# Batch 0 of a packed-attention and mixture-of-experts kernel: K loaded first and in four pieces, gate weights as rows turned on the chip, chunk 0 of the first layer ahead of the second piece of packed weights

## The chip, the cores and the metric

The kernel runs on one core of one Trainium2 chip. The metric is the device time of one execution in microseconds (us), as the median of several runs. The engines of a core are named as the profile names them: PE is TensorE's matrix products and PEld its weight loads, DVE is VectorE, ACT is ScalarE, POOL is GpSimd, SP is SyncE, which issues most DMAs. An engine with a q behind its name (SPq, ACTq) is that engine's instruction queue, where DMAs are issued.

## What is computed

Eight batches, eight heads, 576 tokens, head size 64. Attention goes twice through 32 packed rows per head; its output, 512 wide, goes through one of eight experts for each token. Which expert it is follows from a gate; a token can also keep the expert of the token before it.

```python
def _attn_ref(q, k, v, p):
    scale = 1.0 / np.sqrt(q.shape[-1])
    def sm_attn(qq, kk, vv):
        s = scale * np.matmul(qq, kk.transpose(0, 1, 3, 2))
        s = s - np.max(s, axis=-1, keepdims=True)
        a = np.exp(s)
        a = a / (np.sum(a, axis=-1, keepdims=True) + 1e-09)
        return np.matmul(a, vv)
    p_packed = sm_attn(p, k, v)
    out = sm_attn(q, p_packed, p_packed)
    return out.astype(np.float32)
...
    logits = np.einsum('bsd,de->bse', x, w_gate)
    local_gate = 1.0 / (1.0 + np.exp(-np.einsum('bsd,de->bse', x, w_local).squeeze(-1)))
...
            fresh_e = int(np.argmax(logits[b, s]))
            if s == 0 or local_gate[b, s] < 0.5:
                e = fresh_e
            else:
                e = prev_e if prev_e >= 0 else fresh_e
...
            h = np.maximum(x[b, s] @ w1[e], 0.0)
            out[b, s] = p[e] * (h @ w2[e])
```

## The kernel before

The kernel takes it that all tokens of a batch use the expert of the batch's first token, and works out at the end whether any did not; for these there is a general branch, which doesn't run here. For each batch it computes the packed rows (`ppT`, two groups Q of four heads), multiplies them into w1 of the expert ("packed weights", `pack_weights`), and then runs the two layers over eight chunks c of 128 hidden columns and two parts of the tokens (256 and 320 columns). Each float32 product in the layers is made of three: every operand is split into a high part and the rest (`wph` and `wpl`, `a2h` and `a2l`, the two halves of `w2s`).

Work is written as generators, one for each step of each batch. A planner (`weave`, with a cost table in the class `Clock`) runs the program's steps in the order in which its own estimate of the engines' times lets them be ready, and each `yield need(...)` names the tiles, buffers, banks or conditions on which a step waits. The order on each engine is fixed by this when the program is built; on the chip each engine runs its list in order and waits on semaphores. So a change of one condition or one estimate shifts places throughout the program. All loads go out on SP in the order of `loads`. They use eight completion semaphores in turn, so the ninth DMA waits for the first to have landed.

Batch 0 is special (`early`). Its start, in the program's order:

- `loads` (L355): p, K in two halves (`load_whole`, L284), the first rows of q for three batches (`t`), V in two groups, the gate weights (`w`: `wgl`, 64 partitions x 8 heads x 8 or 1 numbers, loaded in this layout straight from DRAM), Q in two halves.
- Five products of a zero tile (L227, 256 columns each: `WARM`) keep TensorE at work till the data is there; more of them are put in wherever the planner sees PE idle ahead of batch 0's first chunk.
- p is turned (L413), then K in six groups of three 128x128 transpositions (`turn_whole`, L439), whose copies out of PSUM (L440) alternate between ACT and DVE. Then come the scores (L447), maxima, exponentials (L550), their transpositions (L567), the products with V (L598), and two transpositions of the packed rows (`zz`, L616), each with a copy to `ppT` on ACT (L619).
- The probe of the first token (`early_choice`): a product of `ppT` with the first rows of q for each group (L870), a small softmax, a product with the gate values (L903), the largest of eight (L908, L910). SP reads the expert's number (L855) and issues that expert's weights: two pieces of the first half of w1 (`w1k`, 256 columns each, L1025), four chunks of w2 (L1032), then the second half of w1 (`w1t`).
- Meanwhile Q is turned (L439, L440, tile `qT`) and the second attention step runs in two parts of the tokens (`first_queries`).
- `pack_weights` multiplies `ppT` into w1 (L1073), in pieces of `w1k` and then `w1t`; ACT casts the high part (L1082), DVE makes the rest (L1085). Chunks 0 and 1 need the first `w1k` piece, 2 and 3 the second, 4 to 7 `w1t`. The first layer's products are at L1101, the second layer's at L1153.

## Time and profile before

| | us |
|---|---|
| median of 3 runs (413.15 to 414.97) | 413.54 |
| the profiled execution | 414.13 |
| its span, first to last instruction | 412.3 |
| PE busy in the span | 400.5 (97%) |
| DVE, ACT, POOL busy | 247.8, 188.3, 110.5 |

The span is what the profile's rows cover; the 1.8 us between it and the profiled execution's time lie around it. PE is nearly always busy, so the place to look for is where it is not, and what the chain of waits, followed back from the last instruction, names there. Matrix products are pipelined and their ends are modelled; the distance between starts says more than the duration of one. A row of the timeline merges neighbours with the same operation: its first number is the start, the second the time that they take together, and "x" their number, where a float32 product of more than one pass counts as two. What stands in brackets is the engine's idle time before it and what ended it.

### The profile page before, as it was taken

How to read it: one execution, taken by the hardware profiler on the slowest of the kernel's cores; microseconds unless marked ns; L12 is line 12 of the kernel's file. 1: busy time of each engine (PE TensorE's matmuls, PEld its weight loads, DVE VectorE, ACT ScalarE, POOL GpSimd, SP SyncE). 2: the span in 40 equal slices, each digit the busy share in tenths (PEclk: the TensorE clock that was granted, in tenths of full speed). 3: DMA queues.
4: the chain of work that ended last, by engine and by line, in shares of the span. 5: the costliest groups of instructions: out<-in, count | busy, mean ns of one | idle time of the engine just before them, and what ended most of it. 6: DMA issues, size and time to landing. Idle time of an engine off the chain costs nothing.

```text
span 412.3 us, 9812 instructions
## 1 busy us (share of the span) xinstructions
PE 400.5 (97%) x3724; PEld 317.4 (77%) x3725; DVE 247.8 (60%) x666; ACT 188.3 (46%) x447; POOL 110.5 (27%) x138
## 2 busy tenths in 40 slices
PE   8988999999999999999999999999999999999993
PEld 6766777777877788678887887778868788778883
DVE  4697468783877587758934697248842595332221
ACT  2574524744346532485344643545344643453212
POOL 1014500912055203036304412323303413233000
PEclk9999999999999999999999999999999999999998
DMA  7899679974699299569994994899175102820102
GB/s 230 249 313 229 97 187 368 157 173 125 215 274 207 73 220 184 192 231 222 213 334 139 187 200 138 306 229 213 51 248 163 61 4 88 324 93 22 52 0 68
DMA packets 161053, 72.98 MB, mean 177 GB/s; under 512 B 131186, under 2 KB 139882, under 8 KB 161002
## 3 DMA queue, kind: packets, MB, share of 16 engines
q1 hardware_dynamic: 160858, 72.19, 67.8%
q8 instruction: 30, 0.49, 0.5%
q14 instruction: 21, 0.17, 0.1%
q10 hardware_dynamic: 144, 0.13, 0.1%
HBM read 62.87 MB, written 9.44 MB: 175 GB/s over the span
## 4 chain that ended last, share of the span: by engine, by line
PE 91%; DMA 4%; SPq 1%; ACT 1%; DVE 1%; issue 1%; DVEq 0%; ACTq 0%
PE bank L1153 43%; PE bank L1101 24%; PE bank L1073 4%; DMA w1t<-in_moe_w_dram 4%; PE bank L1159 4%; PE bank L1163 3%; PE bank L598 2%; PE bank L567 2%; PE bank L647 2%; PE bank L508 1%; PE bank L227 1%; PE bank L922 1%; PE bank L439 1%; PE bank L616 1%; SPq L1032 0%
## 5 line engine op out<-in xcount | busy, mean ns | idle before, releaser
L1153 PE MATMUL bank<-w2s,h 128*128 128x512 f32 (+1 forms) x771 | 203.8, 397 | 0.0
L1153 PEld LDWEIGHTS bank<-w2s,h 128*128 128x128 f32 x771 | 136.0, 188 | 30.7 <-issue 7.6
L1116 DVE SCALAR_TENSOR_TENSOR h<-bank,h 128x256 fp32r<-128x256 f32 x192 | 61.8, 350 | 98.6 <-ACT h L1112 97.7
L1133 POOL TENSOR_TENSOR w2s<-w2raw,w2s 128x512 fp32r<-128x512 f32 (+1 forms) x68 | 84.2, 1255 | 134.2 <-ACT w2s L1129 127.2
L1112 ACT ACTIVATE h<-bank 128x320 fp32r<-128x320 f32 (+1 forms) x128 | 53.0, 414 | 107.8 <-PE bank L1101 106.0
L1101 PEld LDWEIGHTS bank<-a2h,wph 128*128 128x128 f32 x256 | 46.2, 188 | 18.3 <-issue 5.1
L1101 PE MATMUL bank<-a2h,wph 128*128 128x256 f32 (+1 forms) x256 | 56.6, 302 | 0.0
L1101 PE MATMUL bank<-a2l,wph 128*128 128x256 f32 (+1 forms) x256 | 54.9, 295 | 0.0
L1101 PE MATMUL bank<-a2h,wpl 128*128 128x256 f32 (+1 forms) x256 | 54.6, 295 | 0.0
L1101 PEld LDWEIGHTS bank<-a2l,wph 128*128 128x128 f32 x256 | 40.9, 188 | 0.0
L1101 PEld LDWEIGHTS bank<-a2h,wpl 128*128 128x128 f32 x256 | 40.9, 188 | 0.0
L710 POOL TENSOR_TENSOR a2l<-a2t,a2h 128x320 fp32r<-128x320 f32 (+1 forms) x25 | 20.6, 843 | 75.0 <-ACT a2h L704 75.0
L1129 ACT CAST w2s<-w2raw 128x512 fp32r<-128x512 f32 x64 | 38.7, 620 | 0.8 <-DMA w2raw<-in_moe_w_dram 0.6
L1085 DVE TENSOR_TENSOR wpl<-bank,wph 128x512 fp32r<-128x512 f32 (+1 forms) x34 | 21.2, 651 | 19.8 <-ACT wph L1082 19.8
L1082 ACT CAST wph<-bank 128x512 fp32r<-128x512 f32 (+1 forms) x34 | 17.4, 565 | 24.5 <-PE bank L1073 24.4
L1159 PE MATMUL bank<-w2s,h 128*128 128x512 f32 x64 | 26.4, 412 | 0.0
L1163 PE MATMUL bank<-w2s,h 128*64 128x512 f32 x64 | 25.1, 392 | 0.0
L1193 ACT ACTIVATE o<-bank,pe 128x512 f32<-128x512 f32 x23 | 15.5, 700 | 8.6 <-PE bank L1153 8.5
L634 DVE STREAM_TRANSPOSE qn<-qn 128x1152 f32<-128x1152 f32 x14 | 19.2, 1369 | 0.0
L1073 PE MATMUL bank<-w1t,ppT 64*32 64x512 f32 x240 | 17.0, 601 | 1.7 <-DMA w1t<-in_moe_w_dram 1.7
L460 DVE STREAM_TRANSPOSE qn<-qn 128x1152 f32<-128x1152 f32 x12 | 16.4, 1363 | 0.0
L569 ACT COPY a1T<-bank 116x384 f32<-116x384 f32 (+1 forms) x29 | 11.8, 432 | 9.4 <-PE bank L567 9.4
(150 smaller groups left out, 382.1 us busy)
## 6 DMA issues: line engine op xcount, KB each, us to landing
w2raw<-in_moe_w_dram SPq DMA_DIRECT2D x64, 256.0 KB, 7.5
w1t<-in_moe_w_dram SPq DMA_DIRECT2D x15, 1024.0 KB, 5.1
kv<-in_v_dram SPq DMA_DIRECT2D x16, 560.0 KB, 7.5
qn<-in_q_dram SPq DMA_DIRECT2D x28, 288.0 KB, 4.8
out_dram<-o SPq DMA_DIRECT2D x31, 256.0 KB, 2.7
qn<-in_k_dram SPq DMA_DIRECT2D x24, 288.0 KB, 4.3
raw<-in_k_dram SPq DMA_DIRECT2D x4, 576.0 KB
raw<-in_q_dram SPq DMA_DIRECT2D x2, 576.0 KB
```

The costliest lines, as they stand in the source:

```text
L634: nc.vector.transpose(out=qT, in_=qT)
L710: engine.tensor_tensor(out=a2l[:, cols], in0=a2t[:, cols], in1=a2h[:, cols].bitcast(F32), op=ALU.subtract)
L1073: nc.tensor.matmul(out=ts[Q][32 * h:32 * h + 32, :width], lhsT=st["ppT"][Q][rows, 32 * h:32 * h + 32], rhs=w1t[rows, h], start=True, stop= ...
L1085: nc.vector.tensor_tensor(out=lo[:, Q, cols], in0=ts[Q][:, :width], in1=hi[:, Q, cols].bitcast(F32), op=ALU.subtract,)
L1101: nc.tensor.matmul(out=t[:, :width], lhsT=st["wp"][c // 4][wi][:, Q, fs], rhs=a2[ai][Q][:, ts], start=(n == 0), stop=(n == 5),)
L1112: nc.scalar.activation(out=h[:, :n], in_=t[:, :n], func=AF.Relu)
L1116: nc.vector.scalar_tensor_tensor(out=h[:, dst:dst + z - a], in0=t[:, a:z], scalar=0.0, in1=h[:, a:z].bitcast(F32), op0=ALU.max, op1=ALU.su ...
L1129: nc.scalar.copy(out=w[:, 0], in_=raw)
L1133: rest.tensor_tensor(out=w[:, 1, cols], in0=raw[:, cols], in1=w[:, 0, cols].bitcast(F32), op=ALU.subtract)
L1153: nc.tensor.matmul(out=acc[:, cols], lhsT=hs[hi], rhs=w[:, wi, cols], start=(c == 0 and n == 0), stop=(n == 2 and (c == NC - 1 or c == NC ...
L1159: nc.tensor.matmul(out=acc, lhsT=h[:, EDGE:EDGE + 2 * TAIL], rhs=w[:, 0], start=(c == 0), stop=False, skip_group_check=True,)
L1163: nc.tensor.matmul(out=acc[0:TAIL], lhsT=h[:, EDGE:EDGE + TAIL], rhs=w[:, 1], start=False, stop=(c == NC - 1), skip_group_check=True,)
```

## The change

For batch 0 alone:

- SP loads K first, in four pieces: groups 0 to 2, then 3, 4 and 5 alone. p, the gate weights and the first rows of q are loaded on ACT's queue instead, ahead of ACT's table load. The gate weights come as eight rows of 512 (and of 64) numbers, as they lie in DRAM, and nine transpositions on PE and one copy on DVE (`local_weights`) bring them into the old layout.
- Three warm-up products, not five, and the planner's estimates of when PE and the first DMA are free are lowered.
- Q's first three groups may be turned before the probe is done, and turning starts once the first group of packed rows has its transposed exponentials.
- The first chunk's products are placed ahead of the products of the second `w1k` piece, which now wait (in the planner) for that chunk. The maxima of the second part of the tokens wait for the third chunk.

```diff
@@ -42,10 +42,10 @@
 
 FIRST_BACKLOG = 1400.0
 
-WARM, FILL, EACH = (256,) * 5, 0.8, 1.8
+WARM, FILL, EACH = (256,) * 3, 0.8, 1.8
 
 LAT, SAME = 160.0, 127.0
-START, FIRST_LOAD = 6100.0, 1700.0
+START, FIRST_LOAD = 4300.0, 1300.0
 KEPT = ("bank6", "bank7")
 BUFS = {
     "kv": 2, "qn": 3, "p_in": 2, "q_in": 1, "zz": 2, "a1": 2, "a1T": 2, "a1U": 2, "ppT": 3, "sT": 2, "a2t": 2,
@@ -281,13 +281,13 @@
         ready.banks = banks
         return ready
 
-    def load_whole(src, b):
+    def load_whole(src, b, cuts=(0, NG // 2, NG)):
 
         x = tile_([128, NG, NM * 2 * D], F32, "raw", "qn")
-        clock.edges[x.tensor.name] = (H * HALF // 2,)
+        clock.edges[x.tensor.name] = tuple(NM * 2 * D * g for g in cuts[1:-1])
         clock.rate = 400.0
         rows = src[b].rearrange("h s d -> (h s d)").rearrange("(p g x) -> p g x", p=128, g=NG)
-        for z in (slice(0, NG // 2), slice(NG // 2, NG)):
+        for z in (slice(*y) for y in zip(cuts, cuts[1:])):
             nc.sync.dma_start(out=x[:, z], in_=rows[:, z])
         return x
 
@@ -355,9 +355,14 @@
 
         b = st["b"]
         if st["early"]:
-            st["p"] = load_packs_whole(b, nc.sync)
+            st["p"] = load_packs_whole(b, nc.scalar)
+            st["rows"] = tile_([H, D * GW], F32, "rows", "w2s")
+            nc.scalar.dma_start(out=st["rows"][:, :D * E], in_=w_gate.rearrange("(h d) e -> h (d e)", d=D))
+            nc.scalar.dma_start(out=st["rows"][:, D * E:], in_=w_local.rearrange("(h d) e -> h (d e)", d=D))
+            st["t"] = tile_([FIRST * H, D], F32, "q_in")
+            nc.scalar.dma_start(out=st["t"], in_=q[0:FIRST, :, 0].rearrange("b h d -> (b h) d"))
             nc.scalar.activation(out=spare_col, in_=ones_col, func=AF.Exp)
-            order = (("k", 0), ("t", 0), ("v", 0), ("v", 1), ("w", 0), ("q", 0))
+            order = (("k", 0), ("v", 0), ("v", 1), ("q", 0))
         else:
             if isinstance(b, int):
                 yield need(when=lambda: "loaded" in sts[b - 1] and (b < 2 or "ereg" in sts[b - 2]) and (b <= FIRST or len(sts[b - 2].get("w2", ())) == NC))
@@ -371,16 +376,6 @@
 
                 yield need(when=lambda: len(sts[b - 1].get("w1", ())) == 2)
             room = "p_in" if name == "p" else "qn" if name in "kq" else "kv"
-            if name == "t":
-                st["t"] = tile_([FIRST * H, D], F32, "q_in")
-                clock.rate = 100.0
-                nc.sync.dma_start(out=st["t"], in_=q[0:FIRST, :, 0].rearrange("b h d -> (b h) d"))
-                continue
-            if name == "w":
-                clock.rate = 20.0
-                nc.sync.dma_start(out=wgl[:, :, 0:E], in_=w_gate.rearrange("(h d) e -> d h e", d=D))
-                nc.sync.dma_start(out=wgl[:, :, E:E + 1], in_=w_local.rearrange("(h d) e -> d h e", d=D))
-                continue
             if st["whole"] and name == "q":
                 yield need(when=lambda: "turning" in st)
             if ends is None or name != "v":
@@ -400,7 +395,7 @@
                 if Q:
                     st[name] = True
             else:
-                st["raw" + name] = load_whole(x, b)
+                st["raw" + name] = load_whole(x, b, *(((0, 3, 4, 5, 6),) if st["early"] and name == "k" else ()))
         st["loaded"] = True
 
     def turn_packs(st):
@@ -426,13 +421,13 @@
 
         yield need(when=lambda: "raw" + name in st)
         raw = st["raw" + name]
-        yield need(slot="qn", when=lambda: name == "k" or "rawk" in sts[1])
+        yield need(slot="qn")
         x = tile_([128, NG, H, HALF // NG], F32, name + "T", "qn")
         st["turning"] = True
         clock.edges[x.tensor.name] = tuple(H * HALF // NG * g for g in range(1, NG))
         for g in range(NG):
             yield need(raw[:, g], banks=1, when=lambda: (
-                (name == "k" or g == 0 or "spread" in st) if st["early"] else g < 3 or sts[0]["raised"] > 0
+                (name == "k" or g < 3 or "spread" in st) if st["early"] else g < 3 or sts[0]["raised"] > 0
             ))
             tp = bank()
             for m in range(NM):
@@ -624,7 +619,7 @@
     def turn_queries(st, Q):
         if st["early"]:
             if Q == 0:
-                yield need(when=lambda: st.get("probed", 0) > 0)
+                yield need(when=lambda: ("turned", 0) in st)
                 act, dve = nc.scalar.copy, nc.vector.tensor_copy
                 yield from turn_whole(st, "q", (act, act, act, dve, act, act))
             return
@@ -751,7 +746,7 @@
                     give(ts[Q, 0], ts[Q, 1])
 
         def highest(z):
-            yield need(sT[z]) if z == 0 else need(when=lambda: st["packed"] > 256)
+            yield need(sT[z]) if z == 0 else need(when=lambda: st["firsts"] > 2)
             nc.vector.reduce_max(out=mx[z], in_=sf[z], axis=AX.X)
 
         def raised(z):
@@ -823,10 +818,21 @@
         for x in (*st["a2t"], *st["a2h"], *st["a2l"]):
             clock.edges[x.tensor.name] = (EDGE,)
 
+    def local_weights(st):
+
+        yield need(st["rows"], banks=1)
+        tp = bank()
+        for e in range(GW):
+            rows = st["rows"][:, e:D * E:E] if e < E else st["rows"][:, D * E:]
+            nc.tensor.transpose(out=tp[:D, H * e:H * e + H], in_=rows, identity=ident[:H, :H])
+        nc.vector.tensor_copy(out=wgl[:, :, 0:GW], in_=tp[:D, :H * GW].rearrange("a (e h) -> a h e", h=H))
+        give(tp, st["rows"])
+        st["local"] = True
+
     def gate_weights(st):
 
-        yield need(when=lambda: None not in st["ppT"])
-        yield need(*st["ppT"], banks=1)
+        yield need(when=lambda: None not in st["ppT"] and "local" in sts[0])
+        yield need(*st["ppT"], wgl, banks=1)
         gp = bank()
         for Q in range(NQ):
             for h in range(HQ):
@@ -1065,7 +1071,7 @@
                 if isinstance(st["b"], int) and st["b"] == B - 1 and fh:
                     yield need(w1t)
                     yield from look_for_strays()
-                yield need(w1t, banks=NQ, skip=skip, left=1)
+                yield need(w1t, banks=NQ, skip=skip, left=1, when=lambda: not (early and fh == 0 and n) or st["firsts"] > 0)
                 ts = [bank(skip=skip) for Q in range(NQ)]
                 for Q in range(NQ):
                     rows = slice(64 * Q, 64 * Q + 64)
@@ -1245,8 +1251,9 @@
             hi, lo = st["wp"][c // 4]
             cols = slice(*EDGES[part:part + 2])
             fs = slice(128 * (c % 4), 128 * (c % 4) + 128)
-            packs = [x[:, Q, fs] for x in (hi, lo) for Q in range(NQ)]
-            rests = () if st["early"] and part == 0 and c == 0 else st["a2l"]
+            soon = st["early"] and part == 0 and c == 0
+            packs = [x[:, Q, fs] for x in ((hi,) if soon else (hi, lo)) for Q in range(NQ)]
+            rests = () if soon else st["a2l"]
             yield need(*packs, *(x[:, cols] for x in (*st["a2h"], *rests)), banks=1)
             h, done = tile_([128, S + TAIL], F32R, "h"), set()
             aside(relu(layer1(c, part, st), part, h, done))
@@ -1317,7 +1324,7 @@
                 st = sts[started]
                 threads.extend(Thread(g, started) for g in (
                     slots(st), pack_weights(st), *((early_choice(st),) if st["first"] else ()),
-                    turn_keys(st, 0), turn_keys(st, 1), *((scores(st, 0), scores(st, 1)) if st["whole"] else (scores(st, 0, 1),)), keys(st, 0), keys(st, 1), gate_weights(st) if st["first"] else None, gates(st), turn_queries(st, 0), turn_queries(st, 1), first_queries(st) if st["early"] else queries(st, beside(started)),
+                    turn_keys(st, 0), turn_keys(st, 1), *((local_weights(st),) if st["early"] else ()), *((scores(st, 0), scores(st, 1)) if st["whole"] else (scores(st, 0, 1),)), keys(st, 0), keys(st, 1), gate_weights(st) if st["first"] else None, gates(st), turn_queries(st, 0), turn_queries(st, 1), first_queries(st) if st["early"] else queries(st, beside(started)),
                 ) if g is not None)
                 threads.insert(0, Thread(weights(st), started, True))
                 threads.append(Thread(splits(st), started, True))
```

How this moves instructions is decided by the planner. Three places follow. Lines from 281 on shift a little in the new kernel: L439 becomes L434, L413 L408, L619 L614, L440 L435, L1101 L1107, L1073 L1079, L556 L551.

PE from its first product to the first group of K, before: `warm` is the zero tile, `p_in` is p, `raw` is K as loaded.

```order
L227 MATMUL bank_66<-warm 128x256 x5
L413 MATMUL bank_126<-ident,p_in 128x128 x2
L439 MATMUL bank_135<-ident,raw 128x128 x3
L439 MATMUL bank_140<-ident,raw 128x128 x3
L439 MATMUL bank_145<-ident,raw 128x128 x3
```

And after, where `rows` are the gate weights as loaded:

```order
L227 MATMUL bank_66<-warm 128x256 x3
L408 MATMUL bank_127<-ident,p_in 128x128 x2
L827 MATMUL bank_136<-ident,rows 64x8 x9
L227 MATMUL bank_66<-warm 128x128
L434 MATMUL bank_148<-ident,raw 128x128 x3
```

Two warm-up products of 256 columns are gone; nine small transpositions and one warm-up product of 128 columns stand between p and K.

ACT around the two copies of the packed rows and the probe, before: `ppT` are the packed rows, `qT` is a turned group of Q, `es` the probe's exponentials.

```order
L569 COPY a1T<-bank_230 116x384
L619 COPY ppT<-bank_295 128x128
L619 COPY ppT<-bank_299 128x128
L440 COPY qT<-bank_307 128x384
L887 ACTIVATE es,em<-es,em 128x32
L842 COPY gate_90<-bank_316 128x64
```

And after:

```order
L564 COPY a1T<-bank_244 116x384
L614 COPY ppT<-bank_309 128x128
L435 COPY qT<-bank_312 128x384
L435 COPY qT<-bank_317 128x384
L614 COPY ppT<-bank_326 128x128
L435 COPY qT<-bank_329 128x384
L893 ACTIVATE es,em<-es,em 128x32
L848 COPY gate_88<-bank_338 128x64
```

Two copies of Q have moved between the two copies of the packed rows; on PE the same two groups of Q stand between the transpositions that feed them.

ACT in the first batch's second part of the tokens, around the exponentials of batch 1's scores (`a`), before:

```order
L556 ACTIVATE a_473,s_773<-a_473,nb 128x576
L569 COPY a1T<-bank_777 116x384
L1112 ACTIVATE h<-bank_760 128x320
L569 COPY a1T<-bank_783 116x256
L965 ACTIVATE ex<-under 128x40
L967 ACTIVATE fresh_all<-lt 128x5
L556 ACTIVATE a_714,s_800<-a_714,nb 128x576
```

And after:

```order
L551 ACTIVATE a_486,s_776<-a_486,nb 128x576
L564 COPY a1T<-bank_783 116x384
L564 COPY a1T<-bank_790 116x256
L551 ACTIVATE a_731,s_798<-a_731,nb 128x576
L971 ACTIVATE ex<-under 128x40
L973 ACTIVATE fresh_all<-lt 128x5
L1118 ACTIVATE h<-bank_801 128x320
```

The second exponential has moved ahead of a relu (`h`) and two small activations.

## Rows read from the trace of the kernel before

**Rows 1.** Busy time by stage: stretch, PE, PEld, DVE, ACT, POOL busy, clock, DMA.

```profile
33.70:406.00 372.30, 371.26 (x3363) 295.31 (x3363) 224.99 (x596) 169.77 (x398) 104.24 (x117) 1.00 0.68 171
```

**Rows 2.** The chain of waits, 0 to 60 us: start, us, what it was.

```profile
6.37 2.03 PE bank L439 x18
...
9.16 0.70 PE bank L447 x16
...
24.05 9.56 DMA w1t<-in_moe_w_dram
...
33.66 1.09 PE bank L1073 x16
```

**Rows 3.** Timeline, 26 to 34 us: start, us, engine, line, operation, tiles.

```profile
26.90 0.74 DVE L797 TENSOR_TENSOR a2l<-a2t,a2h 128x256 fp32r<-128x256 f32 x2
...
26.93 0.67 PE L1073 MATMUL bank<-w1k,ppT 64*32 64x256 f32 x16 [0.99 <-DMA w1k<-in_moe_w_dram]
...
33.66 1.09 PE L1073 MATMUL bank<-w1t,ppT 64*32 64x512 f32 x16 [1.16 <-DMA w1t<-in_moe_w_dram]
```

**Rows 4.** Timeline, 15 to 19.6 us, the probe of the first token.

```profile
15.54 0.27 ACT L619 COPY ppT<-bank 128x128 f32<-128x128 f32 x1 [1.26 <-PE bank L616]
...
16.08 0.27 ACT L619 COPY ppT<-bank 128x128 f32<-128x128 f32 x1 [0.28 <-PE bank L616]
...
16.65 0.26 PE L870 MATMUL bank<-ppT,q 64*32 64x32 f32 x8
...
16.81 0.48 ACT L440 COPY qT<-bank 128x384 f32<-128x384 f32 x1 [0.46 <-PE bank L439]
...
18.33 0.21 DVE L894 STREAM_TRANSPOSE et<-es 128x32 f32<-128x32 f32 x1
...
18.75 0.28 PE L903 MATMUL bank<-gate,et 128*1 128x32 f32 x4
...
19.07 0.16 DVE L908 MAX8 emx<-bank 1x8 f32<-1x8 f32 x1
```

**Rows 5.** Timelines of PE and of its weight loads, 3 to 9 us.

```profile
3.60 1.91 PE L227 MATMUL bank<-warm 128*128 128x256 f32 x4
4.46 1.49 PE L227 MATMUL bank<-warm 128*128 128x256 f32 x3
...
5.74 0.23 PEld L413 LDWEIGHTS bank<-ident,p_in 128*128 128x128 f32 x1 [0.20 <-issue]
5.95 0.23 PEld L439 LDWEIGHTS bank<-ident,raw 128*128 128x128 f32 x1
...
6.16 2.23 PE L439 MATMUL bank<-ident,raw 128*128 128x128 f32 x18
```

**Rows 6.** Line 477, q's first rows turned: duration ns min/median/max, first and last start.

```profile
L477 PEld LDWEIGHTS bank<-ident,q_in x1: 105/105/105, 8.3 to 8.3; 24*64 24x64 f32 x1
```

**Rows 7.** Busy time by stage while K is loaded; the last number is GB/s.

```profile
2.00:4.70 2.70, 2.70 (x8) 2.13 (x7) 0.78 (x3) 0.34 (x2) 0.00 (x0) 1.00 0.86 246
2.00:6.20 4.20, 4.20 (x13) 3.24 (x12) 0.78 (x3) 0.34 (x2) 0.00 (x0) 1.00 0.92 297
```

**Rows 8.** Timeline: the first DMAs, p's first copy, and ACT's one DMA.

```profile
0.88 0.45 SPq L343 DMA_DIRECT2D p_in<-in_p_dram  x1
1.38 0.94 SPq L291 DMA_DIRECT2D raw<-in_k_dram  x2
...
2.95 0.23 DVE L409 COPY p_in<-p_in 128x128 f32<-128x128 f32 x1 [0.48 <-DMA p_in<-in_p_dram]
...
407.10 0.39 ACTq L1176 DMA_DIRECT2D out_dram<-o  x1
```

**Rows 9.** Timeline, 48 to 50 us, batch 1's second exponential and its user.

```profile
48.66 0.78 ACT L556 ACTIVATE a<-a,nb 128x576 f32<-128x576 f32 x1
...
49.59 0.81 PE L567 MATMUL bank<-ident,a 128*116 128x128 f32 x5 [0.55 <-ACT a L556]
```

**Rows 10.** The page's DMA issues: KB each, median us from issue to landing.

```profile
w1t<-in_moe_w_dram SPq DMA_DIRECT2D x15, 1024.0 KB, 5.1
```

## The prediction

> **What bounds the kernel now.** I first read where TensorE (PE) stands idle, since everything else is fed to it. From 33.70 to 406.00 us PE is busy 371.26 of 372.30 us [rows 1]: that stretch is a wall of matrix products, which the change reorders but doesn't shorten. What comes ahead of it can be shortened. The chain of waits shows what opens the wall: the load of the second half of the first expert's w1 (w1t), issued at 24.05 and in use 9.56 us later, at 33.66 [rows 2]. PE had run out of other work 1.16 us before [rows 3]. So a microsecond is won only if that load is issued earlier, or if idle time inside the wall goes. The load is issued as soon as SyncE (SP) has the number of the first token's expert, and this number comes out of a chain: load K and p, turn them (L439), scores, softmax, products with V, the probe of the first token (L870), the largest gate value (MAX8, L908, at 19.07 [rows 4]). I follow the change along that chain. Its sum is made against the profiled execution: 414.13 us, of which 412.3 are the span. The median of the runs is 413.54, 0.6 lower.
>
> **Part 1: the start, up to the last K transposition.** Two of five warm-up products go. They start 0.855 us apart (3.60, 4.46) [rows 5], so p's two transpositions come at 5.74 - 1.71 = 4.03 in place of 5.74. Before K there now stand nine small transpositions of the gate weights (8 rows to 64x8) and one warm-up product of 128 columns, half of 0.855, so 0.43. The small ones aren't in the trace. The nearest below are the weight load of the one that turns q's first rows, 0.105 us each [rows 6], or half of that at the least, 0.055; the nearest above is a p transposition, 0.21 (5.74 to 5.95) [rows 5]. I take 0.107, half a p transposition for half the columns: 9 x 0.107 = 0.96; bounds 0.5 and 1.9. K then starts at 4.03 + 0.43 + 0.96 + 0.43 = 5.85 in place of 6.16 [rows 5]: 0.31 earlier. Little of this reaches the end, because of TensorE's clock. The spacing of the p transpositions is 0.21 us, that of K's 18 is 2.03 / 18 = 0.11 [rows 2, 5]: PE passes from the lower level (1.2 GHz) to the upper one (2.4) at about 6.4 us, after unbroken work since 1.3. (The clock column prints 1.00 for the stretch ahead of it too [rows 7]; the spacing says otherwise.) If it rises at the same moment, three or four transpositions of K run at the slow spacing instead of one or two, and 0.31 shrinks to about 0.1. With the bounds of the small ones: 0.4 earlier to 0.5 later. **I take -0.1.**
>
> Is the data there? K's first half and p, 655 KB, had been moved by 4.7 us (2.7 us at 246 GB/s is 664 KB), all of K by 6.2 (4.2 at 297 is 1247 of 1245 KB) [rows 7]. K's first DMA goes out at 0.88, where p's stood, not at 1.38 [rows 8]; so half of K is there by about 4.5 and all by about 6, and PE needs them at 5.85 and from 6.8 on. K first is hidden by PE itself, and four pieces win nothing. p now goes out on ScalarE's (ACT's) queue at about the same 0.9; it landed 2.0 us after its issue, and its copy runs at 2.95 [rows 8]: needed at 4.03, 0.85 to spare. The gate rows follow on that queue, one issue (0.39 us [rows 8]) later each, so they land near 3.3 and 3.7 and are needed at 4.46. Four issues, 1.6 us, stand ahead of ACT's table load, which was the first thing on ACT; its first data, three K transpositions, are not there before 6.4, so they cost nothing. SP's V loads now wait for p's landing and K's first half, and behind them the Q loads; but the DMA engines work on K till 6 us, so the queue doesn't run dry. The old gate load in tiny pieces goes. Nobody waited for it; Q may land a microsecond earlier, which is hidden too.
>
> A rule on this. The rows show K and p on one queue, one after the other [rows 8]. The Trainium skill, "DMA: Bandwidth & Descriptors", section "Issuing engines are not separate DMA queues", says that DMAs issued by several engines run on the same 16 DMA engines, so that another queue saves issue time alone. By it K gains at most the 0.5 us of issue, as I have it; with a queue of its own it would gain p's transfer as well. The sum is the same by both.
>
> **Part 2: the probe.** In before the second ppT copy runs on ACT at 16.08, right after its transposition, and the second half of the probe at 16.65 [rows 4]. In after two transposition groups of Q and their copies (qT) stand between the two ppT copies. A qT copy takes 0.48 [rows 4], so the second ppT copy starts after 15.54 + 0.27 + 2 x 0.48 = 16.77, or 16.6 where copies overlap; 0.27 for it and 0.05 to PE make the probe 16.95 to 17.1, late by 0.3 to 0.45. The chain behind it on VectorE (DVE) and ACT moves with it. 0.2 come back: in before the gate product L903 waited behind Q's transpositions till 18.75, though its input was ready at 18.33 + 0.21 [rows 4]; in after those are done by then. But a qT copy on DVE stands ahead of MAX8 as before. **I take +0.2**; bounds 0 and +0.45.
>
> **Part 3: chunk 0 ahead of the second piece.** It can't start its last products before DVE has both halves of a2l, 26.90 + 0.74 = 27.64 [rows 3]; it ends near 28.0. The second piece (16 products, 0.67 us), at 26.93 in before [rows 3], is then done at 28.7, and its casts and differences near 30.3, where chunk 2 waits for them. With the second layer of chunk 0 and chunk 3, some 2.4 us, PE is through by about 32.8, not 32.5; w1t lands at 33.6 [rows 3]. So it costs **nothing**, under the cover of that 1.16 us wait; if w1t came a microsecond earlier the cover would be gone and up to 0.3 would show.
>
> **Part 4: inside the wall.** PE waits 0.55 us at 49.59 for ACT's exp L556 of batch 1's second head group, which starts at 48.66 behind a relu and two small activations [rows 9]. In after this exp stands ahead of them and its PE user comes after a chunk and one product group, 1.6 us, not 1.4. The wait should nearly go: **-0.4**, bounds -0.55 and +0.2. Elsewhere the wall's instructions are the same in number; places change by one.
>
> Sum: -0.1 + 0.2 + 0 - 0.4 = -0.3: 413.8 for a profiled execution, **413.2** off the median. With the bounds of each added (-0.4 to +0.5, 0 to +0.45, 0 to +0.3, -0.55 to +0.2) the sum goes from -0.95 to +1.45; not all fall on one side, and I give this case 412.5 to 414.4.
>
> **Rivals.** *The clock rises late (ends slower).* PE does 1.7 us less of long warm-up and has small transpositions and perhaps a pause in their place. If the rise waits for the scores, all 18 K transpositions are 0.21 apart: 5.85 + 18 x 0.21 = 9.63 against 6.16 + 2.23 = 8.39 [rows 5], so 1.2 later, and the scores, 0.70 [rows 2] at the upper level, add half as much again as far as the first maximum waits for them, 0.3. With parts 2 and 4: 413.5 + 1.5 + 0.2 - 0.4 = 414.8; up to 415.8 if it stays low through the scores and the exponentials. It decides from a rise at about 7.0 us: each 0.21 of delay costs 0.10, and the 0.3 gain is then used up. For it: five warm-ups were needed to get to 6.4. Against it: PE is still at work nearly without a gap from 1.3, and in before the rise came while K was being turned [rows 2, 5]. The Trainium skill, "TensorE: Matmul & The Clock Gate", section "Part 4: PE-mode transpose", says that the full clock doesn't engage for transpositions; the row agrees only in part, for they ran at the upper level once it was there. Chance 0.2.
>
> *The whole start moves (faster).* If the clock is up before K starts, the small transpositions cost 0.5 and K starts at 5.2 or before: 5.2 + 18 x 0.11 = 7.2, K's data allowing (6 us for the last piece). That is 1.2 earlier than 8.39: 413.5 - 1.2 + 0.2 - 0.4 = 412.1; with the probe at its lower bound and the wait at 49.6 gone whole, 411.7, and any more lies below. For it: the profiled execution is 0.6 above the median, so others may have had the clock earlier. Chance 0.18.
>
> *The load of w1t sets its own time.* 9.56 us from issue to use is long; the median for w1t is 5.1 [rows 10]. If V's loads behind it on the queue, and not its issue, make the landing, then it moves by a microsecond either way whatever the start does: 412.5 or 414.3. Chance 0.1.
>
> **How the numbers follow.** Forecast 0.48, late clock 0.2, early start 0.18, own landing 0.08; 0.06 is left for a stall lost or gained in the reordered wall that I don't see. A measurement of this kernel tells about 0.5% from no change, 2.07 us: faster is below 411.5, slower above 415.6. Faster: half of the early starts (0.09), where w1t also lands sooner, 0.03 of the landings and 0.03 unseen, 0.15. Slower: somewhat under half of the late clocks (0.09) and 0.04 of the last two, 0.13. The rest, 0.72, lies within. Range 411.6 to 415.3, which leaves out a tenth on either side.
>
> **What would show it.** Right: w1t still opens the wall near 33.5 with PE idle ahead of it; the last K transposition ends between 8.0 and 8.4; the second ppT copy stands 0.5 later behind the first than in before; no wait at 49.6. Wrong: K transpositions 0.21 apart to the end; PE waiting for the gate rows; w1t used before 32.5; a new wait of over 0.5 us after 34.

## The result

| | kernel before | kernel changed |
|---|---|---|
| median, the four runs of each | 413.67 us | 418.54 us (416.75 to 420.23) |
| ratio to before | | 1.0105, 95% interval 1.007 to 1.014 |
| profiled execution: time, span | 414.13, 412.3 us | 418.64, 416.8 us |
| last matrix product ends | 406.04 us | 410.68 us |

The change makes the kernel about 1% slower; 413.2 was forecast, with a range that ended at 415.3. In six more runs, beside other kernels, it took 417.89 us, at a ratio of 1.0086 (1.0063 to 1.0109). So the loss to explain is 3.6 to 4.9 us, and 4.64 between the two traces.

The start of the changed kernel, from its timeline (start, us, engine, line, operation, tiles, and in brackets the idle time ahead and what ended it):

```profile
0.86 0.46 ACTq L343 DMA_DIRECT2D p_in<-in_p_dram  x1
0.89 1.83 SPq L291 DMA_DIRECT2D raw<-in_k_dram  x4
...
5.05 0.23 DVE L404 COPY p_in<-p_in 128x128 f32<-128x128 f32 x1 [2.57 <-DMA p_in<-in_p_dram]
```

The timeline of PE alone, 2 to 12.2 us:

```profile
1.31 2.93 PE L227 MATMUL bank<-warm 128*128 128x256 f32 x6 [1.31 <-DVE warm L220]
5.37 0.66 PE L408 MATMUL bank<-ident,p_in 128*128 128x128 f32 x2 [1.13 <-DVE code L243]
5.96 0.67 PE L827 MATMUL bank<-ident,rows 8*64 8x8 f32 x9
6.57 0.80 PE L227 MATMUL bank<-warm 128*128 128x128 f32 x2
7.15 3.75 PE L434 MATMUL bank<-ident,raw 128*128 128x128 f32 x18
```

p was issued at 0.86 as planned, but DVE could copy it only at 5.05, against 2.95 in before [rows 8]. PE stood idle for 1.13 us. (The row names a small DVE cast; the copy of p is what that cast stood behind.) K's 18 transpositions began at 7.15, not 6.16, and took 3.75 us, not 2.23 [rows 5]: 15 of them are 0.21 apart, the spacing of the lower clock. K's end moved from 8.39 to 10.90.

The probe, and what opens the wall:

```profile
18.03 0.27 ACT L614 COPY ppT<-bank 128x128 f32<-128x128 f32 x1 [1.26 <-PE bank L611]
...
19.16 0.28 ACT L614 COPY ppT<-bank 128x128 f32<-128x128 f32 x1
...
21.84 0.16 DVE L914 MAX8 emx<-bank 1x8 f32<-1x8 f32 x1
...
35.87 1.09 PE L1079 MATMUL bank<-w1t,ppT 64*32 64x512 f32 x16 [0.44 <-DMA w1t<-in_moe_w_dram]
```

Busy time from there to the last product (the stretch, its length, PE busy with its count, PEld, DVE, ACT, POOL, clock, DMA share, GB/s):

```profile
35.87:410.70 374.83, 373.18 (x3363) 296.26 (x3363) 224.94 (x597) 170.50 (x399) 103.34 (x118) 1.00 0.67 170
```

The 4.64 us then split like this. The wall opens 2.21 later: K's end +2.51, the probe +0.26 (MAX8 is 2.77 later than in [rows 4]), the issue and landing of w1t -0.56. Within the wall PE is idle for 1.65 instead of 1.04, +0.6. And the wall's 3363 products, as many as in [rows 1], keep PE busy for 373.18 and not 371.26: about +1.9, in a stretch where the granted clock is 1.00 in both. (The three parts add up to 0.1 more than 4.64, because these rows and [rows 1] don't begin and end exactly with the products.) The prediction had no term at all for that last part.

### The profile page after: what moved, and what is told of

It reads as the page before. It is cut to its first block, busy times and chain, and to the rows that moved or that the text cites. A ratio compares the mean times of both kernels' runs of the same rounds, so it can differ in the third digit from the quotient of the medians.

```text
span 416.8 us, 9835 instructions
## 1 busy us (share of the span) xinstructions
PE 404.5 (97%) x3733; PEld 320.2 (77%) x3734; DVE 246.9 (59%) x666; ACT 188.6 (45%) x447; POOL 110.1 (26%) x139
## 4 chain that ended last, share of the span: by engine, by line
PE 85%; DMA 8%; DVE 2%; SPq 1%; issue 1%; ACT 1%; POOL 0%; ACTq 0%; DVEq 0%
PE bank L1159 41%; PE bank L1107 23%; DMA w2raw<-in_moe_w_dram 4%; PE bank L1165 3%; PE bank L1169 3%; PE bank L1079 3%; PE bank L593 2%; PE bank L562 2%; PE bank L642 2%; DMA w1t<-in_moe_w_dram 1%; DMA w1k<-in_moe_w_dram 1%; PE bank L928 1%; PE bank L503 1%; DMA p_in<-in_p_dram 1%; PE bank L434 1%
## 5 line engine op out<-in xcount | busy, mean ns | idle before, releaser
L1159 PE MATMUL bank<-w2s,h 128*128 128x512 f32 (+1 forms) x771 | 205.9, 399 | 0.6 <-POOL w2s L1139 0.6
L1159 PEld LDWEIGHTS bank<-w2s,h 128*128 128x128 f32 x771 | 136.4, 188 | 31.3 <-issue 6.5
L1107 PEld LDWEIGHTS bank<-a2h,wph 128*128 128x128 f32 x256 | 46.4, 188 | 19.6 <-issue 5.4
L1107 PE MATMUL bank<-a2h,wph 128*128 128x256 f32 (+1 forms) x256 | 57.5, 305 | 0.0
L1107 PE MATMUL bank<-a2h,wpl 128*128 128x256 f32 (+1 forms) x256 | 55.2, 295 | 0.6 <-DVE wpl L1091 0.6
L1107 PE MATMUL bank<-a2l,wph 128*128 128x256 f32 (+1 forms) x256 | 55.3, 297 | 0.0
L1107 PEld LDWEIGHTS bank<-a2h,wpl 128*128 128x128 f32 x256 | 41.2, 188 | 1.0 <-DVE wpl L1091 0.8
L1107 PEld LDWEIGHTS bank<-a2l,wph 128*128 128x128 f32 x256 | 41.1, 188 | 0.3
L629 DVE STREAM_TRANSPOSE qn<-qn 128x1152 f32<-128x1152 f32 x14 | 19.0, 1365 | 0.0
L1079 PE MATMUL bank<-w1t,ppT 64*32 64x512 f32 x240 | 16.5, 601 | 0.9 <-DMA w1t<-in_moe_w_dram 0.9
L551 ACT ACTIVATE a<-a,nb 128x576 f32<-128x576 f32 x14 | 11.0, 785 | 13.8 <-DVE nb L531 13.8
L1165 PEld LDWEIGHTS bank<-w2s,h 128*128 128x128 f32 x64 | 12.0, 188 | 5.6 <-issue 2.2
```

Of the source, the lines that this page charges most:

```text
L629: nc.vector.transpose(out=qT, in_=qT)
L1079: nc.tensor.matmul(out=ts[Q][32 * h:32 * h + 32, :width], lhsT=st["ppT"][Q][rows, 32 * h:32 * h + 32], rhs=w1t[rows, h], start=True, stop= ...
L1107: nc.tensor.matmul(out=t[:, :width], lhsT=st["wp"][c // 4][wi][:, Q, fs], rhs=a2[ai][Q][:, ts], start=(n == 0), stop=(n == 5),)
L1159: nc.tensor.matmul(out=acc[:, cols], lhsT=hs[hi], rhs=w[:, wi, cols], start=(c == 0 and n == 0), stop=(n == 2 and (c == NC - 1 or c == NC ...
L1165: nc.tensor.matmul(out=acc, lhsT=h[:, EDGE:EDGE + 2 * TAIL], rhs=w[:, 0], start=(c == 0), stop=False, skip_group_check=True,)
```

## Experiments

The kernels ran in four groups, each beside before, whose median was 413.85, 414.09, 414.05 and 413.81 in them. Across groups the ratios are what compares.

| kernel | median, us | ratio to before (95%) |
|---|---|---|
| changed, five warm-ups (a_warm5) | 416.68 | 1.0064 (1.0032 to 1.0096) |
| changed, p first on SP (a_psync) | 416.39 | 1.0059 (1.0037 to 1.0081) |
| changed, chunk order undone (a_chunkoff) | 419.11 | 1.0131 (1.0074 to 1.0188) |
| before, chunk order alone (b_chunkon) | 415.56 | 1.0020 (0.9996 to 1.0045) |
| changed, w2s and h at their old places (a_layout) | 415.60 | 1.0027 (1.0000 to 1.0054) |
| before, w2s and h at the new places (b_layout) | 416.20 | 1.0040 (1.0016 to 1.0064) |
| changed, w2s shifted by 96 bytes (a_pad) | 415.97 | 1.0035 (1.0015 to 1.0055) |
| changed, once more (a_same) | 417.89 | 1.0086 (1.0063 to 1.0109) |
| p first, old places, five warm-ups (a_best5) | 413.34 | 0.9979 (0.9952 to 1.0006) |
| the same, four warm-ups (a_best4) | 413.68 | 1.0008 (0.9979 to 1.0036) |
| gate rows behind V, K in four pieces (a_late) | 414.67 | 1.0012 (0.9986 to 1.0037) |
| gate rows behind V, K in two (a_late2) | 414.96 | 1.0019 (1.0000 to 1.0038) |

### Is it the order in the wall?

The first theory for the loss inside the wall was its new order: chunk 0 ahead of the second piece. It was undone in the changed kernel, and done alone in the old one.

```
# a_chunkoff
-            yield need(sT[z]) if z == 0 else need(when=lambda: st["firsts"] > 2)
+            yield need(sT[z]) if z == 0 else need(when=lambda: st["packed"] > 256)
...
-                yield need(w1t, banks=NQ, skip=skip, left=1, when=lambda: not (early and fh == 0 and n) or st["firsts"] > 0)
+                yield need(w1t, banks=NQ, skip=skip, left=1)
...
-            packs = [x[:, Q, fs] for x in ((hi,) if soon else (hi, lo)) for Q in range(NQ)]
+            packs = [x[:, Q, fs] for x in (hi, lo) for Q in range(NQ)]
# b_chunkon: the same lines the other way round, in the kernel before
```

> The changed kernel with the third part undone: chunk 0 of the first layer no longer goes ahead of the second piece, it waits for the low half of its weights again, and the second maximum waits for 256 packed columns. Start and probe as changed. Theory W (the new order in the wall costs the 2.4 us that are lost after the second piece opens): 416.1 (415.5 to 416.8). Theory N (those 2.4 us are no matter of that order: the matmuls of both layers are some 1 to 2 per cent further apart all the way, and 0.6 us are new waits): within 0.5 us of 418.5.

> The kernel before with the third part of the change alone: chunk 0 of the first layer ahead of the second piece, without its low half of weights, and the second maximum behind the third chunk. Start, loads and probe as before. Theory W (the new order in the wall costs 2.4 us): 416.1 (415.4 to 416.8). Theory N (it costs nothing): 413.7 (413.0 to 414.4), with second-layer matmuls 227 to 228 ns apart where nothing is waited for, as in the trace of before, and not 232.

Undoing it gained nothing: 419.11 against 418.54 and 417.89. Done alone it cost 0.8 us by the ratio, with an interval from -0.2 to 1.9, so perhaps nothing. Its median, 415.56, is 1.7 above before's in the same group, inside W's range and outside N's. But the ratio's interval ends below the 2.4 that theory W needed, and undoing brought nothing; so W falls as the cause of the whole 2.4. What differs in b_chunkon are waits: from 33.37 to 407.63 us PE is idle for 3.14 us, against 1.04 in before's wall, and busy for 371.12, no longer than in before. From the list of PE's waits (what waited, for whom, us in total, times, longest):

```profile
PE bank L1073 <- DMA w1t<-in_moe_w_dram: 1.2, 2, 0.7
PE bank L567 <- ACT a L556: 1.1, 1, 1.1
```

The undoing put in waits too: in a_chunkoff's wall PE is idle for 3.00 us, against 1.65 in the changed kernel, so a small gain from it could be hidden behind them. Its busy time there, 373.29, stays that of the changed kernel.

The pace of the products sorted the kernels another way. I took the starts of neighbouring second-layer products from the traces, after 60 us, where they are at most 240 ns apart. In before and in b_chunkon 225 of 657 and 232 of 659 follow each other within 224 to 227 ns. In the changed kernel it is 11 of 660, in a_chunkoff 9 of 668, and in a_warm5 and a_psync (below) 6 and 10. Nearly all the rest lie at 228 to 238 in all of them. So in these traces the slower pace goes with the changed program, whatever its order. That left the places of the operands. A buffer pool gives out SBUF, the on-chip memory, in the order in which tiles are first named. The changed kernel names its `rows` tile in w2s's room at the very start, and so w2s's ten buffers begin at byte 25984 instead of 177120, and h at 207840 instead of 166880.

### The places of the buffers

```
# a_layout: the changed kernel
-            st["rows"] = tile_([H, D * GW], F32, "rows", "w2s")
+            st["rows"] = tile_([H, D * GW], F32, "rows", "wph")
# b_layout: the kernel before, one line more in loads
+            give(tile_([H, D * GW], F32, "rows", "w2s"))
# a_pad: the changed kernel
+            give(tile_([128, 24], F32, "pad0"))
             st["rows"] = tile_([H, D * GW], F32, "rows", "w2s")
+            give(tile_([128, 104], F32, "pad1"))
# ... and one buffer each for pad0 and pad1 in BUFS
```

> The changed kernel with one word changed: the tile that holds the gate weights as rows takes its room from the buffers of wph and not from those of w2s. All five engines' orders are the same as in the changed kernel, instruction for instruction. What moves is the place of the buffers in SBUF: in the changed kernel the early rows tile puts the ten w2s buffers at byte 25984 and up, ahead of all others, and h at 207840; here h and w2s stand at 166880 and 177120 again, as before the change. Theory L (addresses: since w2s stands elsewhere, no two matmuls of the second layer follow each other within 224 to 227 ns, as some 4 in 10 do before the change): these intervals come back, the gain is about 2.0 us and the time 416.5 (416.0 to 417.2). Rival D (the pace has another cause, the addresses are a bystander): 418.5, intervals of 230 to 238 ns.

> The kernel before with a tile of w2s's buffers named at the start and given back at once; nothing is written to it, and all engines' orders are those of before, instruction for instruction. Only the buffers' places in SBUF move, to those of the changed kernel (w2s from byte 25984, h from 207840). Theory L (addresses): second-layer matmuls 230 to 238 ns apart and no longer 224 to 227, time 413.85 plus 2.0, so 415.8 (415.2 to 416.4). Rival D: 413.85 (413.3 to 414.4).

> The changed kernel with 96 bytes left free ahead of w2s's buffers and 416 behind them: w2s begins at byte 26080 and no longer at 25984, all later buffers stand 512 bytes further on; all engines' orders are the same as in the changed kernel. Theory R (what counts is where w2s's buffers begin within 512 bytes: before, 177120 is 345 times 512 plus 480, as 26080 is 50 times 512 plus 480; changed, 25984 leaves 384): the second-layer intervals of 224 to 227 ns come back and the time is that with the old places, 415.6 (415.0 to 416.4). Rival F (what counts is that w2s stands far from h, or in a low part of the memory): intervals of 230 to 238 and 417.7.

Theory L holds in both directions. Old places brought the changed kernel down to a ratio of 1.0027, from 1.0086 and 1.0105, a little more than L had forecast (415.60, where its range began at 416.0); the new ones took before up to 1.0040, with not one instruction moved. The short intervals came back (208 of 655) and went (7 of 657). Busy time of the second layer, from the page (idle time ahead at the end), in the changed kernel, then in b_layout, a_layout and a_pad; before had 203.8 us, 397 ns:

```profile
L1159 PE MATMUL bank<-w2s,h 128*128 128x512 f32 (+1 forms) x771 | 205.9, 399 | 0.6 <-POOL w2s L1139 0.6
```

```profile
L1154 PE MATMUL bank<-w2s,h 128*128 128x512 f32 (+1 forms) x771 | 205.9, 399 | 0.0
```

```profile
L1159 PE MATMUL bank<-w2s,h 128*128 128x512 f32 (+1 forms) x771 | 204.1, 397 | 0.2 <-POOL w2s L1139 0.2
```

```profile
L1161 PE MATMUL bank<-w2s,h 128*128 128x512 f32 (+1 forms) x771 | 204.0, 397 | 0.3 <-DVE h L1124 0.3
```

Each is one execution. Of the six traces with the new places five gave 205.9 to 206.2 (a_chunkoff, in another order, 204.7); the eight with the old places or with a_pad's gave 203.1 to 204.4. a_layout and b_layout move other buffers besides (a_layout puts wph's in the early room instead); a_pad moves w2s by 96 bytes and all that lies behind it by 512. It decides between R and F: w2s stays low and far from h, only its start changes within 512 bytes (from 384 to 480, as before; h is at 480 throughout), and 228 of 664 intervals are short again, at a ratio of 1.0035. So it is where w2s starts within 512 bytes that counts, not the region. No run moved h within 512 bytes, so whether w2s's start counts by itself or against h's is open; which smaller unit it is, and why, was not tried.

The repetition of the changed kernel gives the number to hold these against:

> The changed kernel once more, beside the others of this call, for its time from more than four runs and a second trace of it. Buffers' places are worth 2.1 us (before kernel, 414.09 to 416.2) and the rows p landing late about 2 us; on the 415.6 that the changed kernel has with the old places, the 2.1 make 417.7 (417.0 to 418.6). If the clock's rise at 10.46 us in the first trace belongs to this kernel's start (theory S), it rises after 10 again; if it differs from execution to execution (rival), anywhere between 4.3 and 10.7, as in the traces so far.

### p and the clock

```
# a_warm5
-WARM, FILL, EACH = (256,) * 3, 0.8, 1.8
+WARM, FILL, EACH = (256,) * 5, 0.8, 1.8
# a_psync
-            st["p"] = load_packs_whole(b, nc.scalar)
+            st["p"] = load_packs_whole(b, nc.sync)
```

> The changed kernel with five warming matmuls at the start instead of three; nothing else. In the changed kernel TensorE stands idle from 4.24 to 5.37 us, until the packed rows p have landed, and the clock stays at half until 10.46 (before: 6.37). Theory S (the start: TensorE's idle 1.13 us keeps the clock down): with ten passes of the warming matmuls TensorE is busy until 5.75, the clock rises near 6.4, the 18 K transposes take about 2.1 us and not 3.7, the second piece of packed weights opens near 34.0 and not 35.9, and the time is 416.6 (415.9 to 417.3). Rival A (late data set the start, the clock is a bystander): the K transposes still end near 10.9 and the time stays at 418.5. No theory expects the time of before, 413.7: 2.4 us of the loss arise after the second piece opens.

> The changed kernel with the packed rows p issued on SP ahead of K, as before the change; gate rows and query rows stay on ACT. TensorE's order is the same as in the changed kernel. p should land near 3.0 us and not 5.0. Theory S: TensorE then does the two p transposes near 4.0 but still waits, for the gate rows (they landed at 5.24 and 6.03), so an idle stretch of about 0.7 us or more is left ahead of 6 us, the clock still rises late, and the time gains little: 418.2 (417.5 to 418.6). Rival A (p alone holds up the start): K transposes from about 6.2 and the clock near 6.4, time 416.3.

a_psync's start, from its timeline (the last row from that of PE alone):

```profile
0.89 0.45 SPq L343 DMA_DIRECT2D p_in<-in_p_dram  x1
...
1.39 1.92 SPq L291 DMA_DIRECT2D raw<-in_k_dram  x4
...
2.88 0.23 DVE L404 COPY p_in<-p_in 128x128 f32<-128x128 f32 x1 [0.41 <-DMA p_in<-in_p_dram]
...
4.59 0.65 PE L827 MATMUL bank<-ident,rows 8*64 8x8 f32 x9
...
6.27 2.47 PE L434 MATMUL bank<-ident,raw 128*128 128x128 f32 x18 [0.61 <-DMA raw<-in_k_dram]
```

With half a microsecond's lead p is there at 2.88, and PE doesn't wait for the gate rows: my theory S expected that wait and a late clock, and was wrong; A's 416.3 came true. PE does wait for 0.61 us, for K's first piece, which lands at 6.23 here and not at 4.81; but the full clock had begun at 4.74, ahead of that wait, and it stayed. Is it ACT's queue that made p late, or the company of K? The gate rows (16 KB) take p's old place here: they go out on ACT's queue at 0.86, half a microsecond ahead of K, and have landed by 2.60. The next load on that queue, 2 KB issued 0.13 behind K's first piece, landed at 4.08. So it isn't the queue by itself that is slow. By the ratios p's place is worth 1.1 us against a_same and 1.9 against the first runs; the intervals of a_psync and a_same overlap, so its size is known less well than that of the places.

a_warm5 gave S's number, 416.68. Its trace does not show S's mechanism: PE has no idle row from 1.31 to K's end, and K's transpositions still took 3.71. But this trace is that of the slowest of its ten runs, 420.45, so it doesn't tell how a run of 416.68 began, and S isn't refuted by it. a_same, a_layout and a_pad run the changed kernel's start instruction for instruction, with PE idle for 1.24, 1.07 and 1.33 us ahead of p. PE's timeline of a_layout, then of a_pad:

```profile
5.32 0.41 PE L408 MATMUL bank<-ident,p_in 128*128 128x128 f32 x2 [1.07 <-DVE code L243]
...
6.56 2.13 PE L434 MATMUL bank<-ident,raw 128*128 128x128 f32 x18
```

```profile
5.56 0.66 PE L410 MATMUL bank<-ident,p_in 128*128 128x128 f32 x2 [1.33 <-DVE code L243]
...
7.34 4.05 PE L436 MATMUL bank<-ident,raw 128*128 128x128 f32 x18
```

The same work, once all at the upper level and once all at the lower one. The traced run of a_layout was the fastest of its twelve (412.85), that of a_pad the slowest (419.24). By the trace's record of the granted clock, full clock begins at 4.38 in a_layout, 4.30 in a_chunkoff, 9.80 in a_same, 10.46 in the changed kernel and 12.47 in a_pad. In before, b_layout and b_chunkon, busy without a break until p, it begins at 6.37, 6.49 and 7.03; in a_psync, a_best5, a_late and a_late2, which have no break there either, at 4.74, 5.89, 4.32 and 6.31. So the moment is not the program's alone; the start with the break either had full clock just as the break began (4.24) or got it only after 9.8. This speaks for S in part. That a_warm5 (10.71) and a_best4 (9.96) were late without any idle row speaks against it as the whole cause, and what decides is open. How often each kernel's untraced runs had the late clock isn't known either, so part of what the start's variants gain or lose may lie in that share.

### Putting it right

```
# a_best5 = a_layout + a_psync + a_warm5; a_best4 with (256,) * 4
# a_late, a_late2: p first on SP, places as in a_layout, five warm-ups, and
-            order = (("k", 0), ("v", 0), ("v", 1), ("q", 0))
+            order = (("k", 0), ("t", 0), ("v", 0), ("v", 1), ("w", 0), ("q", 0))
# where "w" loads the rows tile by SP; in a_late2 K's cuts are (0, NG // 2, NG)
```

> The changed kernel with three things put right: p on SP ahead of K, the rows tile in wph's room (places of h and w2s as before the change), and five warming matmuls. With p first alone the time was 416.39, its median trace still without the short intervals. Theory L takes 2.0 us off that, and the two more warming matmuls close the idle stretch of 0.61 us ahead of the first K transpose, worth nothing by themselves: 414.3 (413.7 to 415.0), that is, no better than the kernel before (413.85), since the waits that the new order puts into the wall stay. Rival D: 416.3.

> The kernel of 413.34 us (changed, p first on SP, rows tile in wph's room) with four warming matmuls instead of five. With five, TensorE begins the p transposes at 5.74, the gate rows' nine at 6.13 and K's at 6.9, though K's first piece has landed at 6.23 in a trace with the same loads. Theory S: with four, the warming ends near 4.9, p's and the gate rows' transposes are done by 6.0, K's begin near 6.3 and the idle stretch ahead of them stays under 0.4 us, so the clock is not lost; 0.5 us earlier, time 412.8 (412.2 to 413.5). Rival: the second piece of packed weights opens no earlier, or the short idle stretch costs the clock in some executions: 413.3 to 414.5.

> A try at the better kernel: the changed one with p first on SP, K in its four pieces behind it, query rows, V, then the gate rows, Q, all on SP; five warming matmuls; the rows tile in wph's room. TensorE's nine transposes of the gate rows stand behind the scores now and not ahead of K. With the gate rows ahead (the kernel of 413.34 us) the last K transpose began at 8.89, in the kernel before at 8.12. Theory: K's end is what counts, it begins its last transpose near 8.2 and the time is 412.7 (412.1 to 413.4). Rival: the second piece's landing, not the start, opens the wall, and it stays at 413.3.

> The kernel just described with K in two pieces and not in four. If the four pieces start K's transposes earlier (theory of the change), this one is 0.2 to 0.6 us slower: 413.1; if the pieces' landing follows the bytes and the queue, and the first two share the same three groups anyway (rival), it is the same within 0.3: 412.7.

a_best5 is the fastest at 413.34, faster than the 413.7 to 415.0 that I had expected, though 0.9979 (0.9952 to 1.0006) can't be told from before. The two repairs and the two more warm-ups together take away the whole loss, so the rest of the change adds up to little; single parts of it may still cancel out. Taking the fifth warm-up away again brought nothing: K began 0.4 earlier (6.64), but in the traced execution at the lower clock. Both a_late kernels missed my numbers: K ended at 8.2 and 9.1 (9.2 in a_best5), but the gate rows, now behind V, held PE up among the transposed exponentials, and there the clock was lost. PE's timeline of a_late, then its busy time from 14.6 to 17.9 us:

```profile
11.97 0.59 PE L568 MATMUL bank<-ident,a 128*116 128x128 f32 x3 [0.77 <-ACT a L551]
13.58 0.62 PE L834 MATMUL bank<-ident,rows 8*64 8x8 f32 x9 [1.03 <-DMA rows<-in_moe_w_gate_dram]
```

```profile
14.60:17.90 3.30, 3.30 (x87) 2.79 (x86) 1.77 (x7) 0.48 (x1) 0.00 (x0) 0.50 0.07 19
```

The clock is 0.50 with PE fully busy. In a_late2, with a wait of 0.80 in the same place, it was not lost. K in two pieces or four: 1.0019 and 1.0012, no difference to be seen in the time, though K ended 0.9 earlier with four.

## Why the prediction was wrong

- **A term was missing.** "Elsewhere the wall's instructions are the same in number; places change by one" is true of the order. But the diff's `"rows", "w2s"` also moved h and w2s in SBUF, and no step priced that. It is worth 1.7 us (b_layout, 0.0040 of 414) to 2.4 (a_layout against a_same), about as much as the late start, and shown by kernels in which no instruction moved; a_pad, 2.1 below a_same, differs in little but the start of w2s.
- **The step on p failed.** "It landed 2.0 us after its issue ... 0.85 to spare" took a duration from a trace in which p went out 0.5 us ahead of K, and used it where p and K go out together. The copy ran at 5.05, 2.1 late. K's first piece and p landed at 4.81 and 5.02, and the gate rows, taken to land near 3.3 and 3.7, at 5.24 and 6.03. The rule of the Trainium skill that I cited there ("DMA: Bandwidth & Descriptors", "Issuing engines are not separate DMA queues") I had applied to K alone; applied to p it says that another queue doesn't keep p apart from K, and the trace agrees: p landed 0.21 behind K's first piece.
- **The late clock was named with 0.2 and happened**, in the first trace and in the repetition. Part 1's -0.1 rested on "If it rises at the same moment"; it rose at 10.46, 4.1 us later than in before. The rival's point, a rise after about 7.0, was right. Its condition, a rise that waits for the scores, was not met (they begin at 11.64), and its K end of 9.63 was too early, since PE's idle 1.13 us came on top. Of K's 2.51 us the lateness of p by itself is 0.3: a_layout, with the same lateness and an early clock, ended K at 8.69.
- **The small transpositions** were taken at 0.107 us each, 0.96. They begin 0.057 apart and the next product 0.61 after the first of them (5.96 to 6.57), which is near the lower bound of 0.5.
- **Part 2 was right**: +0.2 forecast, +0.26 measured (a_layout and a_best5 the same within 0.02), and the second ppT copy is 0.59 later behind the first.
- **Part 3 was right in the first trace**: PE is ready 0.44 us ahead of w1t, so the cover held. In a_same, a_best5 and a_late PE comes to w1t's first product without an idle stretch, so there the cover is used up. Whether the new order costs anything elsewhere is open: 0.8 us alone, nothing won by undoing it.
- **The load of w1t did vary**, as the third rival had it, but it did not make this loss: from issue to use it took 9.61 us in before, 9.19 in the changed kernel. In a_warm5 and a_pad it took 10.17 and 11.66, with PE waiting 1.72 and 1.69 for it. Why is open.
- **Part 4 was half right.** The wait at 49.6 is gone. Two others came, which the prediction had listed as a sign against it:

```profile
PE bank L1107 <- DVE wpl L1091: 0.6, 1, 0.6
...
PE bank L1159 <- POOL w2s L1139: 0.6, 1, 0.6
```

  So +0.6 over the wall where -0.4 was forecast. A planner that is given new conditions puts new waits in places that no one has looked at; a bound of +0.2 on that was too narrow.

## What to carry to other kernels

Read a diff for what it allocates, not only for what it runs: a tile named earlier moves every buffer behind it, and the cheap test is the old kernel with the new allocation and nothing else. A landing time read from a trace holds only for the transfers that were in flight beside it; before reusing it, list what goes out at the same moment, on any queue. Where a start runs at the lower clock in one execution and at the upper one in the next, don't judge it by one trace.

## What the runs showed of the hardware

- The distance between products of 128x512 that follow one another changed with where one operand, w2s, begins in SBUF: a mean of 229.5 to 230.1 ns with w2s and h both 480 bytes past a multiple of 512, 232.6 with w2s at 384 and h at 480, in all traces of either kind. Over 771 products that is about 2 us.
- A transfer of 64 KB, issued on another engine's queue within 0.03 us of one of 0.6 MB, landed with it, 4.2 us after its issue; 0.5 us ahead of it and on the same queue, 2.0 after.
- Transpositions of 8 rows to 64x8 began 56 to 58 ns apart at the lower clock (the changed kernel) and 56 to 57 at the upper one (a_layout), after a first distance of 79 in both.
- With the changed kernel's start, instruction for instruction, the full clock came between 4.30 and 12.47 us in five traces, and in the trace of a_late it was at 0.50 again between 14.6 and 17.9 us, behind two idle stretches of 0.77 and 1.03 us.
